# Values requested ahead of keys in the rounds, and one unit's keys and values requested by ScalarE

## The chip, the cores and the metric

The kernel runs on one core of a Trainium2 chip. The core has five engines that run their own instruction streams and meet at semaphores: TensorE (PE, matrix products), VectorE (DVE), ScalarE (ACT), GpSimd (POOL) and SyncE (SP), which here only requests transfers. Transfers between the chip's main memory and the core are carried by 16 DMA engines; an instruction on SP, ACT or POOL requests one. The metric is the device time of one execution in microseconds. Three runs of the kernel before took 182.39, 184.64 and 186.26 us; the median is 184.64.

## The reference

Two stages are chained: a retention layer (attention with a decay and no softmax), and a mixture of low-rank adapters on its output.

```python
batch, n_heads, seq, head_dim = 8, 8, 576, 64
scores = scale * q @ k.T                        # per batch and head
Dmat = where(rel >= 0, gamma[h] ** rel, 0)      # rel = row - column
x = ((scores * Dmat) @ v)                       # then to (4608, 512)
...
logits = x @ w_gate                             # (4608, 8)
topk = the 2 largest; w = softmax over the 2
out = x + sum over the 2 of w * (x @ A[e]) @ B[e]     # rank 16
```

## The kernel before

**Units.** The work is cut into 18 units. A full unit is one chunk of 128 positions of two batches with all 8 heads; a sequence of 576 positions has four full chunks and a tail of 64, and a tail unit takes the tails of four batches. Four batches give nine units (units 0 to 7 full, 8 a tail; 9 to 16 full, 17 a tail). Each unit needs its q, k and v, each as two transfers of 256 KB (`load`, L152, with `load_batch`, L139, for one of the two). The buffers rotate: three for q, four each for k and v (L136), so v of unit 4 goes into the buffer of v of unit 0.

**What is done with a unit.** `k_scale` (L223, on POOL) multiplies the keys by powers of the decay. `T_mm` (L243, PE) turns k and q; `k_out`, `q_out`, `qs_out` and `q_turn` (L257 to L287, mostly ACT, q_turn mostly POOL) put the turned tiles where the products need them (kT, M, Qs). `S1_mm` and `S0_mm` (L296, L313, PE) make scores within the chunk, and VectorE masks them (L357, L367). `U_mm` (L388, PE) multiplies keys and values of the chunk to the state (pu), which `U_out` (L404) adds to the state W of the next chunk. `W_values` and `V1_copy` (L209, L216, POOL) copy the values into W and V1. `O_mm` and `O1_mm` (L420, L441, PE) make the output of the unit, `xT_out` (L460, DVE) scales it. The adapters follow: `Z_mm` (L483) gives logits and the low-rank product, `route_a`, `route_s`, `route_b` (L539 to L570) choose and weigh, `X_mm`, `Y_mm`, `B_mm` make the result, `osb_out` (L667) copies it out, `store` (L691) writes it to memory.

**What sets the order.** Nothing reorders instructions: each engine works through its own in the order in which the text issues them, and waits in that order. Units 0 to 3 are written out by hand (L803 to L955); then the loop of L961 runs rounds r = 2 to 16, in which the U product is that of unit r+1, the O products are those of unit r, and the turned k and q those of unit r+2. A request for a buffer is issued by `freed(u, nm)` (L171), which loads unit u + 4 (k, v) or u + 3 (q) where u was, and waits on SP until all readers of the old content are done. In a round SP gets, in this order, k of unit r+5 (L965), v of unit r+4 (L970), the store of unit r-1 (L1002) and q of unit r+5 (L1006), two transfers each. ACT requests a few early transfers itself (L857, L870), in between its copies.

Of the kernel before, what the change touches and what calls it, by code (L numbers as in the profile page):

```python
# [21 lines left out]
def kernel(  # L22
# [10 lines left out]
    nc = tc.nc  # L33
# [91 lines left out]
    def full(u):  # L125
        return units[u][0] < NFULL

    def behind(u):

        c, bp = units[u]  # L130
        if c + 1 < NFULL:
            return u + 2, 0
        return next(x for x in range(NU) if units[x] == (NFULL, bp // 2)), bp % 2
# [5 lines left out]
    def load_batch(u, nm, b, eng=None):  # L139

        c, bp = units[u]
        return (eng or nc.sync).dma_start(
            out=nat[(nm, u)][:, b * H : (b + 1) * H, :],
            in_=srcs[nm][2 * bp + b, :, 128 * c : 128 * c + 128, :].rearrange("h j d -> j h d"),
        )

    def load_open(u, nm):
        nat[(nm, u)] = iop.tile(
            [128, 2 * H, Dh], FP32, tag=nm + "32", name=nm + "32", bufs=NBUF[nm]
        )  # L150

    def load(u, nm):  # L152

        if u >= NU:
            return
        load_open(u, nm)
        c, bp = units[u]
        if full(u):
            for b in range(2):
                load_batch(u, nm, b)  # L160
            return
        for par in range(2):
            b = 4 * bp + 2 * par
            nc.sync.dma_start(
                out=nat[(nm, u)][HALF[par]],
                in_=srcs[nm][b : b + 2, :, 128 * c : 128 * c + 64, :].rearrange(
                    "b h j d -> j (b h) d"
                ),
            )

    def freed(u, nm):  # L171

        load(u + NBUF[nm], nm)
# [7 lines left out]
    def copy(eng, out, in_):  # L181
        if eng is nc.scalar:
            nc.scalar.copy(out=out, in_=in_)  # L183
        else:
            eng.tensor_copy(out=out, in_=in_)  # L185

    def add(eng, out, a, b):
        eng.tensor_tensor(out=out, in0=a, in1=b, op=ALU.add)  # L188
# [5 lines left out]
    def heads(tl, p):  # L194

        v4 = tl.rearrange("p (b a o) d -> p b a o d", b=2, o=2)
        return [v4[:, b, :, p ^ b, :] for b in range(2)]

    def W_open(u):
        n = 1 if full(u) else 2  # L200
        st[u]["W"] = [
            wk.tile([128, 2, 2, HP, Dh], FP32, tag=f"W{x}", name=f"W{x}", bufs=(5, 2)[x])
            for x in range(n)
        ]
        if units[u][0] == 0:
            for p in range(2):
                (nc.vector if u < 2 else nc.gpsimd).memset(st[u]["W"][0][HALF[p], p], 0.0)

    def W_values(eng, u, ps=(0, 1)):  # L209
        vt = nat[("v", u)]  # L210
        for x, w in enumerate(st[u]["W"]):
            for p in ps:
                for b, src in enumerate(heads(vt[HALF[x]], p)):
                    copy(eng, w[HALF[1 - p], p, b], src)
# [8 lines left out]
    def k_scale(eng, u, bs=slice(0, 2)):  # L223
        c = units[u][0]
        kt = nat[("k", u)].rearrange("p (b h) d -> p b h d", b=2)[:, bs]
        eng.tensor_tensor(  # L226
            out=kt, in0=kt,
            in1=gv[:, c, :].unsqueeze(1).unsqueeze(3).broadcast_to(
                (128, bs.stop - bs.start, H, Dh)
            ),  # L230
            op=ALU.mult,
        )

    def T_open(u, nm, tag):
        s = st[u]
        s["p" + nm] = bank(tag, [128, 2, HP, 2, 64], name=f"pt_{nm}")
        if nm == "q":
            s["M"] = wk.tile([128, 2, 2, HP, 128], FP32, tag="M", name="M", bufs=3)
            s["Qs"] = wk.tile([128, HP, 2, 64], FP32, tag="Qs", name="Qs", bufs=2)
        else:  # L240
            s["kT"] = wk.tile([128, 2, HP, 2, 64], FP32, tag="kT", name="kT", bufs=2)
# [29 lines left out]
    def q_turn(eng, u, p):  # L271

        s = st[u]
        copy(
            eng, s["M"][HALF[p], p, 1],
            s["Qs"][HALF[1 - p]].rearrange("p a r i -> p a (r i)"),
        )
# [126 lines left out]
    def U_out(u):  # L404
        s = st[u]
        us, x = behind(u)
        if "W" not in st[us]:
            W_open(us)
        new, old = st[us]["W"][x], s["W"][0]
        if units[u][0] == 0:  # L410
            for p in range(2):
                copy(nc.scalar, new[HALF[p], p], s["pu"][HALF[p]])
            return
        add(nc.vector, new[LO, 0], s["pu"][LO], old[LO, 0])
        pn = wk.tile([128, 2, HP, Dh], FP32, tag="pn", name="pn", bufs=2)
        copy(nc.scalar, pn[HI], s["pu"][HI])
        add(nc.gpsimd, new[HI, 1], pn[HI], old[HI, 1])
# [23 lines left out]
    def O1_mm(u):  # L441
        s = st[u]
        if not full(u):
            return
        vt = nat[("v", u)]
        for hp in range(HP):
            for b in range(2):
                for ho in range(2):
                    p = ho ^ b
                    vv = s["V1"][:, b, hp, :] if p == 0 else vt[HI, b * H + 2 * hp + ho, :]  # L450
                    mm(  # L451
                        s["px"][HALF[ho], b, hp, HI],
                        lhsT=vv,
                        rhs=s["S1"][HALF[p], b, hp, :],
                        start=False,
                        stop=True,
                        skip_group_check=True,
                    )
# [21 lines left out]
    def Z_open(u, tag="F"):  # L480
        st[u]["pz"] = bank(tag, [128, 2, ER + E], name="pz")
# [70 lines left out]
    def route_s(u, ns=(0, 1)):  # L552
        s = st[u]
        for n in ns:
            nc.scalar.activation(
                out=s["sg"][:, n, :], in_=s["pz"][:, n, ER : ER + E], func=AFT.Sigmoid,
                bias=s["ns"][:, n : n + 1], scale=2.0,
            )
# [310 lines left out]
    k_out(nc.scalar, 1)  # L869
    load_batch(2, "q", 0, nc.scalar)  # L870
    load_batch(2, "q", 1)
    for nm, u in (("v", 2), ("k", 3), ("q", 3), ("v", 3)):
        load(u, nm)
    freed(0, "k")
    freed(0, "v")
    T_open(1, "q", "R")
    T_mm(1, "q")
    freed(1, "q")
    q_out(nc.vector, 1, 0)
    q_out(nc.scalar, 1, 1)  # L880
    qs_out(nc.scalar, 1)
    for p in range(2):
        q_turn(nc.scalar, 1, p)
    W_values(nc.gpsimd, 1)
    V1_copy(nc.gpsimd, 1)
    Z_open(0)
# [5 lines left out]
            S0_mask(1, p, slice(b, b + 1))  # L892
    S1_mask(1)
    U_mm(1)
    freed(1, "k")
    U_out(1)
    k_scale(nc.gpsimd, 2)
    nc.gpsimd.dma_start(out=Bcat, in_=moe_B.rearrange("e r d -> (e r) d"))
    W_values(nc.gpsimd, 2)
# [1 line left out]
    k_scale(nc.gpsimd, 3)  # L901
    O_mm(1, "A")
    O1_mm(1)
    freed(1, "v")
    route_a(0)
    route_s(0)
    for b in range(2):
        xT_out(1, slice(b, b + 1))
    route_b(0)
# [51 lines left out]
    for r in range(2, END):  # L961
        nxt, nn = r + 1, r + 2
        if full(nxt):
            U_mm(nxt, "E" if r > 2 else "F")
        freed(nxt, "k")  # L965
        if full(nxt):
            U_out(nxt)
        O_mm(r)
        O1_mm(r)
        freed(r, "v")  # L970
        if full(nxt):
            xT_out(r)
        else:
            for b in range(2):
                xT_out(r, slice(b, b + 1))
        if full(nxt):
            S1_mm(nxt, "R")
            S1_mask(nxt)
        S0_mm(nxt)
        for p in range(2):  # L980
            S0_mask(nxt, p)
        X_mm(r - 1)
        zT_out(r - 1)
        Z_open(r)
        Z_mm(r)
        route_a(r)
        early = nn < NU and not full(nn)
        if not early:
            Y_mm(r - 1, "R")
        if nn < NU:  # L990
            if "W" not in st[nn]:
                W_open(nn)
            T_open(nn, "k", "A")
            T_mm(nn, "k")
            k_out(nc.scalar, nn)
        if early:
            Y_mm(r - 1, "R")
        route_s(r)
        B_mm(r - 1)
        osb_open(r - 1)  # L1000
        osb_out(nc.vector if nn < NU else nc.scalar, r - 1)
        store(r - 1)  # L1002
        if nn < NU:
            T_open(nn, "q", "S")
            T_mm(nn, "q")
            freed(nn, "q")  # L1006
            q_out(nc.scalar, nn, 0)
            q_out(nc.scalar, nn, 1)
            qs_out(nc.scalar, nn)
            W_values(nc.gpsimd, nn)  # L1010
            if full(nn):
                V1_copy(nc.gpsimd, nn)
            for p in range(2):
                q_turn(nc.gpsimd, nn, p)
            if nn + 1 < NU:
                k_scale(nc.gpsimd, nn + 1)
            if r < 2 * NFULL and r % 2 == 0:
                gx_of(r // 2 + 1)
        route_b(r)
# [81 lines left out]
```

## Time and profile before

| | |
|---|---|
| median of three runs | 184.64 us |
| the profiled execution | 181.67 us |
| its span (first to last recorded work) | 179.9 us |
| bytes moved, mean rate | 39.00 MB, 217 GB/s |
| TensorE clock granted, mean | 0.991 of full speed |
| transfers of v, k, q from issue to landing, median (SP's) | 4.9, 4.8, 5.2 us |
| start of the first round's U product (unit 3) | 33.79 us |
| start of the U products of units 9 to 16 | 87.19, 96.06, 105.11, 114.16, 123.27, 132.32, 141.75, 151.50 us |

The profile was taken from one execution, which was faster than the median of the other runs. Times in its rows are in microseconds from the start of the span. A row of a timeline gives start, length, engine, line, operation and operands, and in brackets how long the engine had stood idle before it and what ended that. SPq and ACTq are requests for transfers: their length is how long the issuing engine was held by the request, not how long the transfer took. The chain of work that ended last is followed back from the last instruction, at each step to what released it.

### The profile page before, as it was taken

What the parts mean: (1) busy time and instruction counts of PE and PEld (TensorE: products, weight loads), DVE (VectorE), ACT (ScalarE), POOL (GpSimd) and SP (SyncE); (2) the same over time, 40 slices, a digit from 0 to 9 for tenths busy, and PEclk for the clock granted to TensorE, in tenths of its full rate; (3) what the DMA queues carried; (4) which work ended last, traced back from release to release, by engine and by line L of the source; (5) the groups of instructions that cost most, each with busy time, mean ns of one, the idle gap of its engine ahead of it and who ended that gap; (6) DMA issues with size and microseconds to landing.
All of it is one profiled execution on the core that took longest, in us unless ns stands there. A gap on an engine that the chain in (4) does not pass through costs nothing.

```text
span 179.9 us, 9354 instructions
## 1 busy us (share of the span) xinstructions
PE 172.6 (96%) x4126; PEld 157.0 (87%) x4126; DVE 129.9 (72%) x236; ACT 77.5 (43%) x158; POOL 121.9 (68%) x208
## 2 busy tenths in 40 slices
PE   7999999999999999999999999999999998999990
PEld 5799988989999999988989999999998997989960
DVE  6586475788696869687595878787777767587860
ACT  0743644926262625261818170707171625243330
POOL 7990956597979597878985659595869492992000
PEclk9999999999999999999999999999999999999996
DMA  4999998998989798999989988899999788843126
GB/s 118 281 266 255 249 213 189 231 219 181 260 205 272 193 256 228 249 245 272 242 239 209 266 191 217 229 232 234 236 275 231 184 195 244 232 159 120 47 101 207
DMA packets 119368, 39.00 MB, mean 217 GB/s; under 512 B 114320, under 2 KB 114720, under 8 KB 119328
## 3 DMA queue, kind: packets, MB, share of 16 engines
q1 hardware_dynamic: 113360, 36.51, 81.7%
q10 hardware_dynamic: 5792, 1.75, 4.1%
q8 instruction: 32, 0.52, 1.2%
q0 software_dynamic: 176, 0.15, 0.6%
q14 instruction: 8, 0.07, 0.1%
HBM read 29.09 MB, written 9.44 MB: 214 GB/s over the span
## 4 chain that ended last, share of the span: by engine, by line
PE 91%; DMA 3%; DVE 2%; issue 0%; DVEq 0%
PE pz L487 19%; PE px L432 18%; PE pu L395 9%; PE ps L322 8%; PE pt_k L248 6%; PE px L451 6%; PE po L620 5%; PE pt_q L248 5%; PE ps L304 4%; PE po L605 4%; DMA v<-in_v_dram 3%; PE pf L723 3%; PE pzt L587 2%; DVE M L373 2%; PE pa L514 1%; PE ps L338 1%
## 5 line engine op out<-in xcount | busy, mean ns | idle before, releaser
L185 POOL COPY W<-v 64x256 f32<-64x256 f32 x78 | 29.2, 394 | 21.8 <-DMA v<-in_v_dram 18.7
L373 DVE TENSOR_TENSOR M<-ps,tri 64x1024 f32<-64x1024 f32 (+1 forms) x34 | 37.3, 1097 | 4.7 <-PE ps L322 4.0
L487 PE MATMUL pz<-AW,xT 128*128 128x136 f32 x288 | 37.7, 284 | 0.0
L432 PE MATMUL px<-M,W 128*64 128x128 f32 (+1 forms) x640 | 35.4, 263 | 0.4 <-DVE M L373 0.4
L487 PEld LDWEIGHTS pz<-AW,xT 128*128 128x128 f32 x288 | 34.6, 190 | 0.4
L226 POOL TENSOR_TENSOR k<-k,pack 128x1024 f32<-128x1024 f32 (+1 forms) x18 | 32.5, 1806 | 2.7 <-issue 1.1
L183 ACT COPY kT<-pt_k 128x1024 f32<-128x1024 f32 x17 | 17.3, 1016 | 37.6 <-PE pt_k L248 37.6
L432 PEld LDWEIGHTS px<-M,W 128*64 128x64 f32 x640 | 31.8, 137 | 0.8 <-issue 0.6
L185 POOL COPY M<-Qs 64x512 f32<-64x512 f32 x34 | 20.7, 609 | 12.1 <-ACT Qs L183 9.5
L470 DVE TENSOR_TENSOR xT<-px,gx 128x1024 f32<-128x1024 f32 x11 | 13.5, 1225 | 16.2 <-PE px L451 14.6
L185 DVE COPY osb<-po 128x1024 f32<-128x1024 f32 (+2 forms) x18 | 19.2, 1075 | 6.9 <-PE po L620 5.4
L596 ACT COPY zT<-pzt 128x256 f16<-128x256 f16 (+1 forms) x19 | 6.9, 361 | 36.9 <-PE pzt L587 36.9
L183 ACT COPY M<-pt_q 64x512 f32<-64x512 f32 x35 | 20.2, 577 | 1.5 <-PE pt_q L248 0.6
L395 PE MATMUL pu<-v,k 128*64 128x64 f32 x512 | 18.9, 226 | 0.6 <-DMA v<-in_v_dram 0.6
L322 PE MATMUL ps<-Qs,kT 64*64 64x128 f32 (+1 forms) x304 | 18.3, 260 | 0.0
L395 PEld LDWEIGHTS pu<-v,k 128*64 128x64 f32 x512 | 16.5, 137 | 2.0 <-DMA v<-in_v_dram 0.4
L322 PE MATMUL ps<-M,kT 64*64 64x128 f32 (+1 forms) x304 | 18.2, 259 | 0.0
L188 POOL TENSOR_TENSOR W<-pn,W 64x512 f32<-64x512 f32 x12 | 15.2, 1270 | 4.0 <-ACT pn L183 3.1
L322 PEld LDWEIGHTS ps<-M,kT 64*64 64x64 f32 x304 | 15.0, 134 | 0.3
L322 PEld LDWEIGHTS ps<-Qs,kT 64*64 64x64 f32 x304 | 14.9, 134 | 0.0
L248 PEld LDWEIGHTS pt_k<-ident,k 64*128 64x128 f32 x272 | 9.9, 138 | 3.2 <-issue 2.9
L185 POOL COPY V<-v 64x256 f32<-64x256 f32 x32 | 11.9, 399 | 0.7
(75 smaller groups left out, 297.5 us busy)
## 6 DMA issues: line engine op xcount, KB each, us to landing
v<-in_v_dram SPq DMA_DIRECT2D x36, 256.0 KB, 4.9
q<-in_q_dram SPq DMA_DIRECT2D x35, 256.0 KB, 5.2
out_dram<-osb SPq DMA_DIRECT2D x34, 256.0 KB, 4.8
k<-in_k_dram SPq DMA_DIRECT2D x33, 256.0 KB, 4.8
k<-in_k_dram ACTq DMA_DIRECT2D x3, 256.0 KB, 4.6
An<-in_moe_A_dram ACTq DMA_DIRECT2D x1, 256.0 KB, 4.4
q<-in_q_dram ACTq DMA_DIRECT2D x1, 256.0 KB, 4.9
out_dram<-osb ACTq DMA_DIRECT2D x2, 128.0 KB, 2.5
```

Source lines behind the costliest of these rows:

```text
L183: nc.scalar.copy(out=out, in_=in_)
L185: eng.tensor_copy(out=out, in_=in_)
L188: eng.tensor_tensor(out=out, in0=a, in1=b, op=ALU.add)
L226: eng.tensor_tensor(out=kt, in0=kt, in1=gv[:, c, :].unsqueeze(1).unsqueeze(3).broadcast_to((128, bs.stop - bs.start, H, Dh)), op=ALU.mult,)
L248: mm(ps[:, r, hp, b, :], lhsT=src[HALF[r], b * H + 2 * hp : b * H + 2 * hp + 2, :], rhs=ident[HALF[r], 64 * r : 64 * r + 64], is_transpose ...
L322: mm(s["ps0"][HALF[1 - p], b, hp, sl], lhsT=s["kT"][HALF[ho], x, hp, b, :], rhs=Q_of(u, b, ho, hp, sl), start=(hp == 0 and x == 0), stop=True,
L373: nc.vector.tensor_tensor(out=s["M"][sl, p, bs].rearrange("p b a i -> p (b a) i"), in0=s["ps0"][sl, bs].rearrange("p b a i -> p (b a) i"), ...
L395: mm(s["pu"][HALF[p], b, hp, :], lhsT=nat[("k", u)][:, h, :], rhs=nat[("v", u)][:, h, :], start=(hp == 0 and b == 0), stop=True, skip_grou ...
L432: mm(s["pxb"][b][HALF[ho], hp, sl], lhsT=s["W"][x][:, p, b, hp, :], rhs=s["M"][:, p, b, hp, sl], start=(hp == 0 and x == 0), stop=True, sk ...
L451: mm(s["px"][HALF[ho], b, hp, HI], lhsT=vv, rhs=s["S1"][HALF[p], b, hp, :], start=False, stop=True, skip_group_check=True,)
L470: nc.vector.tensor_tensor(out=s["xT"][:, bs].rearrange("p b a i -> p b (a i)"), in0=s["px"][:, bs].rearrange("p b a i -> p b (a i)"), in1= ...
L487: mm(s["pz"][:, n, :], lhsT=s["xT"][:, n, dt, :], rhs=AW[:, dt, :], start=(dt == 0), stop=(dt == HP - 1), skip_group_check=True,)
```

## The change

Two things are moved, and no work is added or taken away. In the rounds, the request for the values of unit r+4 stands ahead of that for the keys of unit r+5; both now stand behind the O products. In the part written out by hand, the keys and values of unit 3 are requested by ScalarE and no longer by SyncE: the two transfers of the keys behind its q copies of unit 1, one of the values behind the state copies of unit 1 (`U_out`), the other behind the sigmoids of unit 0 (`route_s`). SP's requests that stood between (k, v of unit 4, q of unit 4, k and v of unit 5) are written in one group behind `route_s(0)`, in the order v4, k4, q4, v5, k5; before it was k4, v4, q4, k5, v5.

```diff
@@ -869,18 +869,18 @@
     load_batch(2, "q", 0, nc.scalar)
     load_batch(2, "q", 1)
-    for nm, u in (("v", 2), ("k", 3), ("q", 3), ("v", 3)):
-        load(u, nm)
-    freed(0, "k")
-    freed(0, "v")
     T_open(1, "q", "R")
     T_mm(1, "q")
-    freed(1, "q")
     q_out(nc.vector, 1, 0)
     q_out(nc.scalar, 1, 1)
     qs_out(nc.scalar, 1)
     for p in range(2):
         q_turn(nc.scalar, 1, p)
+    load_open(3, "k")
+    for b in range(2):
+        load_batch(3, "k", b, nc.scalar)
+    load(2, "v")
+    load(3, "q")
     W_values(nc.gpsimd, 1)
...
     U_mm(1)
-    freed(1, "k")
     U_out(1)
+    load_open(3, "v")
+    load_batch(3, "v", 0, nc.scalar)
     k_scale(nc.gpsimd, 2)
...
     O1_mm(1)
-    freed(1, "v")
     route_a(0)
     route_s(0)
+    load_batch(3, "v", 1, nc.scalar)
+    freed(0, "v")
+    freed(0, "k")
+    freed(1, "q")
+    freed(1, "v")
+    freed(1, "k")
     for b in range(2):
         xT_out(1, slice(b, b + 1))
...
@@ -962,12 +968,13 @@
         if full(nxt):
             U_mm(nxt, "E" if r > 2 else "F")
-        freed(nxt, "k")
         if full(nxt):
             U_out(nxt)
         O_mm(r)
         O1_mm(r)
+
         freed(r, "v")
+        freed(nxt, "k")
         if full(nxt):
             xT_out(r)
```

## The prediction

> **What bounds the kernel now.** I read the profile's page first, then the waits, the chain of work that ended last, and the timelines of SP, POOL, ACT and PE around the places that the diff touches.
>
> ```profile
> PE 172.6 (96%) x4126; PEld 157.0 (87%) x4126; DVE 129.9 (72%) x236; ACT 77.5 (43%) x158; POOL 121.9 (68%) x208
> ...
> DMA  4999998998989798999989988899999788843126
> ...
> PE 91%; DMA 3%; DVE 2%; issue 0%; DVEq 0%
> ```
>
> TensorE is busy for 172.6 of 179.9 us and carries 91% of the chain. The DMA row stands at 8 or 9 tenths from the second slice to the thirty-first: the transfers are almost as full as TensorE. So reordering requests cannot remove work of either; it can only remove the moments in which TensorE stands for a transfer. The waits say which those are (columns: total us, times, longest):
>
> ```profile
> POOL W L185 <- DMA v<-in_v_dram: 18.7, 13, 4.0
> ...
> DVE osb L185 <- DMA out_dram<-osb: 1.4, 3, 0.7
> ...
> PE pu L395 <- DMA v<-in_v_dram: 0.6, 2, 0.3
> ```
>
> In the rounds only the values (v) are late: POOL stands for them 13 times (its W copies, off the chain), and PE's U product (pu, L395) twice. No row has PE standing for k or q. The chain, in order of time, and PE's own rows at the worst place:
>
> ```profile
> 28.30 1.08 PE pu L395 x32
> ...
> 29.60 0.62 PE ps L304 x32
> ...
> 32.57 0.72 PE pt_k L248 x16
> ...
> 114.16 1.15 PE pu L395 x32
> ...
> 132.32 1.08 PE pu L395 x32
> ...
> 141.75 1.21 PE pu L395 x32
> ...
> 145.87 6.22 DMA v<-in_v_dram
> 152.14 1.04 PE pu L395 x28
> ```
>
> ```profile
> 150.50 0.68 PE L248 MATMUL pt_q<-ident,q 64*128 64x64 f32 x16
> 151.50 0.34 PE L395 MATMUL pu<-v,k 128*64 128x64 f32 x4 [0.33 <-DMA v<-in_v_dram]
> 152.14 1.04 PE L395 MATMUL pu<-v,k 128*64 128x64 f32 x28 [0.30 <-DMA v<-in_v_dram]
> ```
>
> An undisturbed U block takes 1.08 us after the q turn before it. That of unit 16 should have ended at 150.50 + 0.68 + 1.08 = 152.26 and ended at 152.14 + 1.04 = 153.18: 0.92 lost. The block at 141.75 lost 1.21 - 1.08 = 0.13, that at 114.16 lost 0.07. Late values cost TensorE 1.12 us in this execution. It is little, but they land on the edge in every one of these rounds, so anything that slows the transfers goes into the time.
>
> **Part 1, the rounds: values ahead of keys.** A round requests two transfers each of k[r+5], v[r+4], a store and q[r+5], in that order. SP's rows (start, length, for the pair):
>
> ```profile
> 94.80 2.68 SPq L142 DMA_DIRECT2D k<-in_k_dram  x2
> 97.58 2.18 SPq L142 DMA_DIRECT2D v<-in_v_dram  x2
> ...
> 104.47 2.23 SPq L142 DMA_DIRECT2D k<-in_k_dram  x2
> ...
> 141.25 3.87 SPq L164 DMA_DIRECT2D k<-in_k_dram  x2
> 145.22 1.41 SPq L142 DMA_DIRECT2D v<-in_v_dram  x2
> ```
>
> Nothing is added or removed: 4 requests of a round change places. These are k12 and v11 of round 7, k13 of round 8, k17 and v16 of round 12. SP goes from one to the next without a gap and is far behind its own program: v11 is released by round 7, whose PE work ended near 87, and goes out at 97.58. So freeing is no longer what holds a request; the queue is, and the later release of v (it needs the O products of unit r, k only U) makes no new SP wait while SP lags. If that lag were gone, v would hold k, store and q behind it by about one O block, which costs nothing as the values would then be early.
>
> Values gain the keys' place: 97.58 - 94.80 = 2.78 us for v11, 145.22 - 141.25 = 3.97 for v16. Unit 16's second half landed at 145.87 + 6.22 = 152.09; 3.97 earlier is 148.1, and TensorE asks at 151.18: 3 us to spare. The losses of 0.92 + 0.13 + 0.07 go: -1.12 us.
>
> Keys lose the values' place: 2.2 us for k12, 1.5 for k17. Who waits for keys first is POOL's scaling:
>
> ```profile
> 24.05 1.17 POOL L185 COPY W<-v 64x256 f32<-64x256 f32 x3 [0.70 <-DMA v<-in_v_dram]
> 25.27 0.75 POOL L185 COPY V<-v 64x256 f32<-64x256 f32 x2
> 27.12 1.90 POOL L226 TENSOR_TENSOR k<-k,pack 128x1024 f32<-128x1024 f32 x1 [1.10 <-issue]
> ...
> 108.60 1.90 POOL L226 TENSOR_TENSOR k<-k,pack 128x1024 f32<-128x1024 f32 x1
> ...
> 155.40 1.90 POOL L226 TENSOR_TENSOR k<-k,pack 128x1024 f32<-128x1024 f32 x1
> ```
>
> ```profile
> k<-in_k_dram SPq DMA_DIRECT2D x33, 256.0 KB, 4.8
> ```
>
> k12's second request goes out by about 96.2 and by the median of 4.8 us lands near 101; unit 12 is scaled at 108.60: 7.6 to spare, 5.4 after. k17 lands near 143.2 + 6 = 149 against 155.40: 6 to spare, 4.7 after. Cost nothing, under a cover of 4 to 5 us; if that were gone, each late us would pass to the k turn on PE. Stores and q keep their places. Next late is then the values again (2 to 4 us spare), then the stores.
>
> **Part 2, the fourth unit's keys and values on ScalarE's queue.** Four requests leave SP (k3, v3) and go to ACT: two behind the turned q copies, one behind the W copies, one behind the sigmoids. ACT's rows:
>
> ```profile
> 11.95 0.47 ACTq L142 DMA_DIRECT2D k<-in_k_dram  x1
> ...
> 16.79 0.37 ACTq L142 DMA_DIRECT2D q<-in_q_dram  x1
> ...
> 19.23 1.25 ACT L183 COPY M<-Qs 64x512 f32<-64x512 f32 x2
> 21.94 1.17 ACT L183 COPY W<-pu 64x512 f32<-64x512 f32 x2 [1.46 <-PE pu L395]
> 24.22 0.43 ACT L555 ACTIVATE sg<-pz,ns 128x8 f32<-128x8 f32 x2 [1.11 <-DVE ns L547]
> 25.79 1.01 ACT L183 COPY kT<-pt_k 128x1024 f32<-128x1024 f32 x1 [1.14 <-PE pt_k L248]
> ...
> 27.89 0.59 ACT L183 COPY Qs<-pt_q 128x512 f32<-128x512 f32 x1
> ```
>
> An ACT request takes 0.37 to 0.47 us. Two (0.94) go into the gap of 1.46, one into 1.11, one into 1.14: cost zero, hidden by waits that ACT has anyway. The buffers are the fourth of four, never used, so the requests wait for nothing. SP's early order becomes v2, q3, v4, k4, q4, v5, k5; before it had these rows:
>
> ```profile
> 19.98 3.16 SPq L142 DMA_DIRECT2D k<-in_k_dram  x2
> 23.25 2.78 SPq L142 DMA_DIRECT2D q<-in_q_dram  x2
> 26.07 3.03 SPq L142 DMA_DIRECT2D v<-in_v_dram  x2
> ```
>
> v3 goes out near 23.1 and 24.7 instead of 26.07. k3 now travels beside v2 instead of behind it. Lower bound: v2 lands as before, at 24.05 where POOL's copies resume. Upper bound: its last 24.05 - 20.48 = 3.57 us take twice as long, 27.6. TensorE wants v2 at 28.30; POOL would then copy until 27.6 + 1.17 + 0.75 = 29.5 and scale k3 until 31.4, ahead of its turn at 32.57: covered at both ends, by 0.7 us at the worse. I take zero. The moved releases (v4, k4, q4, v5, k5) only change program text on a queue that is behind; their buffers are free before SP arrives.
>
> What two queues do for the rate no row shows directly; the nearest:
>
> ```profile
> 9.00:16.25 7.25, 7.25 (x190) 6.88 (x188) 5.98 (x9) 1.95 (x4) 4.18 (x8) 1.00 1.20 270
> 16.25:25.10 8.85, 8.49 (x211) 7.70 (x208) 4.35 (x9) 5.55 (x11) 6.09 (x12) 1.00 1.05 224
> ```
>
> With An and half of k2 on ACT's queue the stretch of 9 to 16 us moved 270 GB/s; that of 16 to 25, with one early ACT request, 224. If ACT's requests raised 8.5 us from 224 to 270, SP would be 8.5 x 46 / 224 = 1.7 us further on for good; if the engines are full either way, 0. The share of busy engines was above 1 in both stretches, which is nearer to full: I take 0 and leave 1.7 to the range. [...]
>
> **The sum.** The profiled execution took 181.67 (span 179.9 and 1.77 around it): 181.67 - 1.12 = 180.55. The median of the three runs, 184.64, lies 2.97 above it. The program's arithmetic is the same in each run, so the excess is in something that varies, and what varies in the trace are the transfers (a pair of requests takes from 1.41 to 3.87 us in the rows above). If all 2.97 is late values, 2.8 or more of it comes back, since the values are 2.78 to 3.97 earlier: 184.64 - 1.12 - 2.8 = 180.7. If none: 183.5. Without a row that decides I take about the middle, 182.2.
>
> **The rivals.** *More than that comes back:* the excess is all late values, or ACT's queue adds its 1.7 us of lead. Time 180.5. For it: the values sit on the edge from unit 11 on. Against: the equal work for the engines.
> *The wait only changes its name:* the transfers as a whole set the pace, and a slow run is then held by the stores, which keep their place (VectorE already stood 3 times for them, 1.4 us), or by keys, which come later. TensorE gets back almost nothing: 184.6. Against: the spare of 4 to 5 us for keys.
> *Slower:* ACT's queue is as clogged as SP's, and a request holds ACT as long as it can hold SP:
>
> ```profile
> L142 SPq DMA_DIRECT2D v<-in_v_dram x32: 367/930/2136, 5.7 to 145.9; - x32
> ```
>
> At the longest, 2.14 us, from 20.48: two requests to 24.76, W copies to 25.93, third to 28.07, sigmoids to 28.5, fourth to 30.64. The kT copy would start there and not at 25.79, Qs would end at 28.48 + 4.85 = 33.33, and S1 of unit 2, at 29.60 now, starts 3.7 late. With the gain of 1.12: 184.64 - 1.12 + 3.7 = 187.2. It decides from the point where kT is 1.12 + 1.12 = 2.24 late (the first 1.12 is the spare between Qs and S1), about 1.5 us a request. Against it: ACT's own rows of 0.37 and 0.47, taken while SP's pair rows were long.
>
> **How the numbers follow.** Forecast 0.50 (182.2, its own range 180.9 to 183.6); more 0.22; new name 0.18; slower 0.10. Two per cent, about what a measurement of this kernel tells from no change, puts the bounds at 180.95 and 188.33. Faster: the 0.22 and 0.03 of the forecast, 0.25. Slower: half of the last rival, whose price may come on a run without the gain, 0.05. The same: 0.70. The range, 180.0 to 185.2, leaves out the last rival and the low end of the first.
>
> **What would show it.** Right: no pu row with a wait for v from unit 11 on, U blocks of 1.08; POOL's 18.7 us of waits for v down to a few; on SP the v pair ahead of the k pair; k scaling with no wait; ACT requests under 0.6 us, kT of unit 2 still near 25.8; the 9 us pace of the rounds unchanged. Wrong: pu or W copies waiting as before, pt_k or pt_q waiting for transfers, VectorE's osb copy waiting for stores, ACT requests above 1.5 us, or a median that stays at 184 with a profile free of waits, which would say that the excess was never late values.

## The result, and the profile after

The changed kernel takes 184.6 us (median of 20 executions, 181.86 to 186.74), the kernel before beside it on the same chip 183.11 us (20 executions, 179.83 to 186.26): a ratio of 1.0127, with an interval of 1.009 to 1.0165. It is 1.3% slower; 182.2 us, 1.3% below the 184.64 us of before, was forecast. The ratios here and below leave out every execution more than 1.5% above the fastest of its kernel, here 10 of the 20 of the changed kernel and 11 of the 20 of the kernel before; by the medians of all executions the ratio is 184.6 / 183.11 = 1.008. The profiled execution took 184.25 us with a span of 182.5, against 181.67 and 179.9 before.

The page of the changed kernel first: busy time, transfers, queues, chain by engine.

```profile
PE 172.3 (94%) x4126; PEld 156.8 (86%) x4126; DVE 131.4 (72%) x236; ACT 77.6 (43%) x158; POOL 121.7 (67%) x208
...
DMA  5997999998899999989998999999999997303135
...
q1 hardware_dynamic: 109200, 35.46, 77.9%
q10 hardware_dynamic: 9952, 2.80, 6.6%
q8 instruction: 32, 0.52, 1.2%
...
PE 91%; DMA 2%; issue 2%; DVE 2%; SPq 0%; DVEq 0%
```

TensorE's busy time is nearly the old one (172.6 before), so its idle time grew from 179.9 - 172.6 = 7.3 to 182.5 - 172.3 = 10.2 us. One entry of the chain has grown: "issue" went from 0% to 2%. The page of the profile defines it as time in which an engine waited for nothing that the profile shows. The row of queue 8 (packets, MB, share of 16 engines) looks negligible; its packets turn out to land just ahead of where TensorE's stops end.

The waits of the changed kernel (total us, times, longest):

```profile
POOL M L185 <- ACT Qs L183: 24.3, 12, 3.4
...
POOL W L185 <- DMA v<-in_v_dram: 7.7, 2, 6.0
...
PE pa L514 <- issue: 1.5, 1, 1.5
...
PE ps L304 <- issue: 1.2, 2, 0.8
```

POOL's waits for values fell from 18.7 us in 13 places to 7.7 in 2, and no row has the U product (pu) wait for a transfer. That is what the first part was forecast to do. SP's rows show the order swapped, values ahead of keys:

```profile
94.30 2.68 SPq L142 DMA_DIRECT2D v<-in_v_dram  x2
97.02 2.96 SPq L142 DMA_DIRECT2D k<-in_k_dram  x2
...
137.62 3.55 SPq L142 DMA_DIRECT2D v<-in_v_dram  x2
141.26 2.38 SPq L164 DMA_DIRECT2D k<-in_k_dram  x2
```

The chain in order of time answers to the one shown of before:

```profile
14.76 1.52 issue
...
35.80 1.08 PE pu L395 x32
...
45.11 1.08 PE pu L395 x32
...
48.66 0.82 issue
...
59.16 0.35 issue
...
145.29 1.08 PE pu L395 x32
...
154.31 1.08 PE pu L395 x32
```

The last two U blocks now begin 154.31 - 145.29 = 9.02 us apart and are 1.08 long; before they began 151.50 - 141.75 = 9.75 apart, and the second, with its gaps, took 153.18 - 151.50 = 1.68. So the late values are gone. But the block that began at 141.75 begins at 145.29: more than came back at the end was lost long before, most of it at 14.76 (1.52), 48.66 (0.82) and 59.16 (0.35). Here is TensorE at the first two:

```profile
14.04 0.71 PE L514 MATMUL pa<-An,sel 64*128 64x128 f32 x8
16.28 0.94 PE L514 MATMUL pa<-An,sel 64*128 64x128 f32 x13 [1.52 <-issue]
...
48.38 0.28 PE L304 MATMUL ps<-M,kT 64*64 64x64 f32 x2
49.48 0.27 PE L304 MATMUL ps<-M,kT 64*64 64x64 f32 x1 [0.82 <-issue]
```

TensorE stops in the middle of a run of products of one kind, for 1.52 and 0.82 us, and the profile names no operand that it waits for. The stop at 14.76 cannot come from the change, for no request that the change moves has been reached by then (the first, ACT's for k3, stands at 20.92). It varies from execution to execution: three of the four further profiles of the same kernel (e3, e12, e15) do not have it, and one (e17) has 0.4 us of it.

**What TensorE waits for.** I took the 32 packets of queue 8 out of the trace (16,384 bytes each), numbered them from 0 (packet n goes with border n), and counted TensorE's pairs of weight load and product from the start. The idle times stand at pairs 219 + 126.6 n, n a whole number, 253 loads and products apart. TensorE has 8,344 rows in the trace, 8,252 loads and products and 92 others, mostly semaphore instructions; with these counted too, from 0, the four stops of the changed kernel in the lines below stand at rows 450, 1218, 1985 and 2497, which is 450 + 256 n within a row (n = 0, 3, 6, 8). I call these places borders. Lines worked out so (us; "gap" is the distance of the pair from the one before it, about 0.05 when undisturbed):

```
kernel         packet  border n-1   packet from .. to    pair  starts   gap   start - packet end
before              3     25.72      27.56 ..  28.51      600   31.72   0.09   3.22
before             24    131.59     133.87 .. 134.79     3260  136.20   0.37   1.40
before             26    142.03     143.18 .. 144.66     3514  146.07   0.21   1.41
after               0                13.91 ..  14.87      219   16.29   1.80   1.42
after               3     27.39      31.42 ..  32.30      598   33.79   0.48   1.49
after               6     44.07      46.52 ..  47.99      976   49.48   1.09   1.49
after               8     54.92      56.60 ..  58.19     1230   59.51   0.62   1.33
```

Each stop ends 1.3 to 1.5 us after a packet has landed, and where a packet landed 3.2 us ahead there was no stop. The page names queue 8 "instruction", and in these two profiles none of its packets lands less than 1.3 us before TensorE goes on at the packet's border. So I take a packet of queue 8 for the next 256 instructions of TensorE; no row names what is in it. In the two profiles it starts 0.2 to 4.0 us behind the previous border and takes 0.88 to 1.85 us. Between two borders lie 3.6 to 7.3 us; where it is about 4, the packet has no more than 2 us to spare. The kernel before stops at such borders too: of its rows here, two did, for 0.5 us together beyond the 0.05.

**The balance of the two profiles.** At each border I took the gap beyond the smallest that any profile of this study has there, where a packet landed less than 1.6 us ahead. In sum that is 3.97 us in the changed kernel (1.72 at pair 219, 0.40, 1.05, 0.59, and two small ones) and 0.70 in the kernel before. 3.97 - 0.70, less the 1.12 of late values, is 2.15 of the 2.6 us by which the spans differ; the rest I did not trace.

### The profile page after: what moved, and what is told of

Same layout as the page of the kernel before. It is cut to its first block, busy times and chain, and to the rows that moved or that the text cites. A ratio compares the mean times of both kernels' runs of the same rounds, so it can differ in the third digit from the quotient of the medians.

```text
span 182.5 us, 9352 instructions
## 1 busy us (share of the span) xinstructions
PE 172.3 (94%) x4126; PEld 156.8 (86%) x4126; DVE 131.4 (72%) x236; ACT 77.6 (43%) x158; POOL 121.7 (67%) x208
## 4 chain that ended last, share of the span: by engine, by line
PE 91%; DMA 2%; issue 2%; DVE 2%; SPq 0%; DVEq 0%
PE pz L487 19%; PE px L432 17%; PE pu L395 9%; PE ps L322 9%; PE pt_k L248 6%; PE px L451 5%; PE po L620 5%; PE pt_q L248 5%; PE ps L304 4%; PE po L605 4%; DMA q<-in_q_dram 2%; PE pzt L587 2%; DVE M L373 2%; PE pa L514 1%; PE ps L338 1%
## 5 line engine op out<-in xcount | busy, mean ns | idle before, releaser
L395 PE MATMUL pu<-v,k 128*64 128x64 f32 x512 | 18.4, 225 | 0.0
```

The costliest lines, as they stand in the source:

```text
L395: mm(s["pu"][HALF[p], b, hp, :], lhsT=nat[("k", u)][:, h, :], rhs=nat[("v", u)][:, h, :], start=(hp == 0 and b == 0), stop=True, skip_grou ...
```

## The experiments

**The theories.** With the two profiles in hand I had these: *rounds* (moving the values costs something that the profile hides), *ScalarE's queue* (four requests from a second queue crowd the transfers, or hold ACT), *early order* (v4 ahead of k4), *instruction packets* (TensorE's own instructions come late beside full data queues, and the change makes this worse), and *chance* (a single profile of each kernel tells nothing). The last column counts the requests for unit 3 that ACT issues.

| run | kernel | median us | before beside it | ratio | interval | ACT's |
|---|---|---|---|---|---|---|
| e1 | rounds swapped alone | 180.79 | 181.05 | 0.9993 | 0.9961 to 1.0026 | 0 |
| e2 | hand-written part alone | 183.1 | 181.05 | 1.0064 | 1.0023 to 1.0105 | 4 |
| e3 | changed kernel again | 183.51 | 181.05 | 1.0141 | 1.0092 to 1.019 | 4 |
| e4 | kernel before again | 181.37 | 181.05 | 1.0006 | 0.9969 to 1.0043 | 0 |
| e5 | ACT's requests alone | 182.36 | 181.04 | 1.0113 | 1.0073 to 1.0152 | 4 |
| e6 | early order alone | 181.62 | 181.04 | 1.004 | 1.0001 to 1.0078 | 0 |
| e7 | changed, few stores | 181.92 | 181.04 | 1.0035 | 0.9989 to 1.008 | 4 |
| e8 | before, program shifted | 187.54 | 181.04 | 1.0379 | 1.0345 to 1.0413 | 0 |
| e9 | changed, nothing by ACT | 181.18 | 181.9 | 0.9997 | 0.9958 to 1.0037 | 0 |
| e10 | keys alone by ACT | 181.84 | 181.9 | 0.9985 | 0.9939 to 1.0031 | 2 |
| e11 | values alone by ACT | 180.96 | 181.9 | 0.9953 | 0.9921 to 0.9985 | 2 |
| e12 | changed kernel, third profile | 182.23 | 181.9 | 1.0056 | 1.0017 to 1.0095 | 4 |
| e13 | rounds swapped, values by ACT | 180.95 | 181.25 | 0.9976 | 0.9942 to 1.0011 | 2 |
| e14 | values alone by ACT, again | 181.56 | 181.25 | 0.9997 | 0.9957 to 1.0037 | 2 |

Four further profiles, one execution each: the changed kernel 182.61 (e15) and 182.1 (e17), the kernel before 180.55 (e16) and 180.43 (e18).

### Which part costs: e1 to e4

e1 swaps the rounds alone:

```diff
             U_mm(nxt, "E" if r > 2 else "F")
-        freed(nxt, "k")
         if full(nxt):
...
         O1_mm(r)
+
         freed(r, "v")
+        freed(nxt, "k")
```

> The rounds part alone (values ahead of keys), the hand-written part as before. Theory A (the early requests on ScalarE's queue hold up TensorE in the first 60 us; the rounds part does what was forecast): faster than before by 0.5 to 1.5 us, no U product waits for values from unit 11 on, U of unit 4 near 43. Theory B (values ahead of keys is what costs): slower than before by 1 to 2 us, with new stalls after 60 us.

e2 has the hand-written part of the change alone, and the rounds as before.

> The hand-written part alone (keys and values of unit 3 from ScalarE, the releases regrouped), the rounds as before. Theory A: slower than before by 2 to 3 us, TensorE idle without a releaser several times before 60 us, U of unit 4 near 45. Theory B: like before within 0.5 us.

e3 and e4 are the changed kernel and the kernel before, profiled once more.

> The changed kernel once more, for a second profile. If its idle time of 1.5 us at 14.8 us, which lies ahead of every instruction that the change touches, belongs to this program, it is there again; if it is chance of one execution, it is gone, and U of unit 4 comes about 1.6 us earlier than the 45.1 of the first profile. Time 1 to 2 us above before under both theories.

> The kernel before once more, for a second profile and as a measure of what a repetition moves: ratio 1 within 0.5%. Theory A: few and short idle times of TensorE without a releaser before 60 us (under 0.5 us in sum).

The rounds cost nothing and bring nothing: 0.9993, neither the gain of 0.5 us or more nor the loss of 1 us or more that the two theories named. The hand-written part is slower, 1.0064, and its interval leaves 1 out. The whole is again slower than before, 1.0141. The second profile of the kernel before (e4) shows why the swap brings nothing; its waits, and SP's request for the values of unit 16:

```profile
POOL W L185 <- DMA v<-in_v_dram: 4.4, 2, 4.0
...
PE ps L304 <- issue: 1.0, 1, 1.0
```

```profile
137.50 2.88 SPq L142 DMA_DIRECT2D v<-in_v_dram  x2
```

The kernel before, unchanged, waits for values in 2 places here and not in 13; both lie early, and no U product waits. The values of unit 16 were requested at 137.5 us and not at 145.2. The third and fourth profile of before (e16, e18) have no U product waiting for values either, nor have the seven profiles of other kernels that keep the rounds as they were (e2, e5, e6, e8, e10, e11, e14). The late values that I costed at 1.12 us were those of one execution in eleven.

### ScalarE's requests or the order: e5 and e6

e5 has ACT's four requests, and SP's releases in the order of before. e6 has everything on SP, with v4 ahead of k4 and v5 ahead of k5. e5 differs from e2 in this:

```diff
     load_batch(3, "v", 1, nc.scalar)
-    freed(0, "v")
     freed(0, "k")
+    freed(0, "v")
     freed(1, "q")
-    freed(1, "v")
     freed(1, "k")
+    freed(1, "v")
```

> Keys and values of unit 3 requested by ScalarE as in the change, the other early requests in the order of before (k4, v4, q4, k5, v5), rounds as before. If the second queue is what costs: slower than before by 1 to 2 us, as the whole early part was. If the order of the early requests costs: like before within 0.5 us.

e6, against the kernel before:

```diff
-    freed(0, "k")
     freed(0, "v")
+    freed(0, "k")
...
     U_mm(1)
-    freed(1, "k")
     U_out(1)
...
     freed(1, "v")
+    freed(1, "k")
```

> All early requests stay on SyncE; only the order v4, k4 and v5, k5 of the change in place of k4, v4 and k5, v5; rounds as before. If the second queue costs: like before within 0.5 us. If the order costs: slower by 1 to 2 us.

ACT's requests alone cost 1.0113, about what the whole change costs. The order alone gives 1.004, with an interval that begins at 1.0001 and so only just leaves 1 out, and as part of e9 below it costs nothing. So the cost lies with ACT's four requests.

### The instruction packets: e7 and e8

e7 leaves out the stores of units 1 to 13 of the changed kernel, so that fewer transfers are in the queues:

```diff
-        store(r - 1)
+        if r > 14:
+            store(r - 1)
```

> The changed kernel without the stores of units 1 to 13 (their rows of the output are not written): 26 of 36 output transfers fewer, all of TensorE's work kept. If TensorE's idle times without a releaser are its own instructions arriving behind data transfers: they all but vanish (under 0.5 us in sum after 50 us), the packets that fetch instructions start within 1 us of the block before, and the time falls to 180 to 181 us on a chip where the changed kernel takes 183.5. If the idle times have another cause: they stay, and the time stays within 1 us of the changed kernel.

e8 adds pairs of products ahead of everything, so that the borders fall on other work of the kernel before:

```diff
-    fill(5, "F")
+    fill(20, "F", 64)
```

> The kernel before with its 5 wide warm-up products replaced by 20 narrow ones of about the same time in sum, which puts 30 more pairs of weight load and product ahead of all else: every later instruction lies 30 pairs further on in TensorE's program. If the idle times without a releaser come at borders of 256 instructions of that program, they still come at pairs 219 + 126.6 k counted from the start, so 30 pairs earlier in the work than before. If they belong to a place in the work (a wait the profile does not name), they stay at the same work. Time within 0.5% of before under both.

From the packets and pairs as above:

```
kernel               packet  border n-1   packet from .. to    pair  starts   gap   start - packet end
e8 (before, shifted)      5     41.09      43.76 ..  44.68      850   46.14   0.63   1.46
e8 (before, shifted)     19    111.41     113.21 .. 114.14     2626  115.54   0.41   1.39
e7 (few stores)          15     87.92      89.42 ..  91.29     2119   92.61   1.01   1.32
e7 (few stores)          24    133.51     135.18 .. 136.34     3260  137.88   0.13   1.53
```

In e8 all work stands 30 pairs later in the program, and the stops are again at 219 + 126.6 n (850 is 219 + 126.6 x 5 less 2, 2626 is 219 + 126.6 x 19 plus 2). They belong to the place in the program, not to the work there. In time, e8 was a miss: I expected no change beyond the added pairs, and its first U product began 5.7 us later (16.53 and not 10.81). The first filling products, which took 8.80 us and not 4.64, make up 4.2 of it. Why they took longer isn't known, and e8's time is not used for anything.

e7 decides nothing. Its ratio to the kernel before is 1.0035, where the changed kernel has 1.0127, 1.0141 and, below, 1.0056, but its interval overlaps that of the last, and 181.92 us misses the 180 to 181 expected. Behind 50 us its borders cost 1.1 us and not the 0.5 expected at most: at 92.6 us it stops for 1 us as others do. From 93 us on they cost 0.1 us in sum, but three of the five profiles of the changed kernel (the result's, e12, e17), with all their stores, have no more there: 0 to 0.1. That data transfers hold the packets back is not shown; leaving out 26 of the 36 output transfers also frees buffers and SP.

### How many requests by ScalarE: e9 to e14

e9 is the whole change, with all of unit 3 requested by SP again:

```diff
-    load_open(3, "k")
-    for b in range(2):
-        load_batch(3, "k", b, nc.scalar)
     load(2, "v")
+    load(3, "k")
     load(3, "q")
+    load(3, "v")
...
-    load_open(3, "v")
-    load_batch(3, "v", 0, nc.scalar)
...
-    load_batch(3, "v", 1, nc.scalar)
```

> The change without ScalarE: all four requests of unit 3 back on SyncE (v2, k3, q3, v3, v4, k4, q4, v5, k5), values ahead of keys in the rounds. Theory A (ScalarE's second queue is the whole cost): like before within 0.5%, 3.1 to 3.3 transfers in flight from 16 to 30 us, no idle time of TensorE at a code border before 60 us. Theory C (the order in the rounds and in the start costs too): slower by 0.7% or more.

e10 is e2 with the values back on SP, e11 is e2 with the keys back on SP.

> Only the keys of unit 3 by ScalarE, its values by SyncE, rounds as before. If the cost is more transfers in flight ahead of TensorE's instructions: slower by about half of what the whole early part cost (0.3 to 0.7%), with 3.7 to 4 in flight from 16 to 30 us. If the cost is ScalarE held by its fourth request: like before within 0.3%, because no request stands ahead of the kT copy.

> Only the values of unit 3 by ScalarE, its keys by SyncE, rounds as before. The second half of the values still waits on ScalarE ahead of the kT copy. If that hold is the cost: slower by 0.5 to 1.1%, kT of unit 2 later than 26 us. If the number in flight is: 0.3 to 0.7%, with kT where it was.

> The changed kernel a third time, as a control on the same chip: 1.2 to 1.5% above before. Its profile should again show above 4 transfers in flight from 16 to 30 us and the fetches of instructions of that stretch landing later than in the kernel before (2.5 us behind the border).

e13 is e11 with the rounds swapped; e14 is e11 once more.

> The change with the keys of unit 3 back on SyncE: values of unit 3 by ScalarE, values ahead of keys in the rounds. If the parts add up as measured: 0.3 to 0.6% faster than before. If only the number in flight counts (3.8 in the start): like before.

> The values of unit 3 alone by ScalarE, repeated. If the gain of 0.5% of the first time is real: ratio 0.993 to 0.998. If chance: 0.998 to 1.002 and the interval holds 1.

Without ACT's requests the change costs nothing: 0.9997. With two of them, keys or values, it also costs nothing. e11 looked like a small gain (0.9953), but its repetition e14 gives 0.9997 and e13 0.9976: no gain is established, and no version beats the kernel before. Neither account in the expectations of e10 and e11 came out: 3.8 transfers were in flight in both at no cost, and in e11 ACT was not held (kT of unit 2 at 25.83 us). With all four and all stores, each of the five comparisons (the result, e2, e3, e5, e12) lies above 1 with its whole interval, from 1.0056 to 1.0141. By the medians of all executions the five are 1.002 (e12) to 1.014 (e3). So the loss comes with the four requests together; that is shown, its size only roughly. Why, is less well shown.

e12 was a miss: 0.56% and not the 1.2 to 1.5% expected. It is the third profile of the changed kernel, and has 0.55 us at borders and a span of 179.0, less than the first profile of the kernel before. The loss isn't there in each execution.

### More profiles of the same two kernels: e15 to e18

> The changed kernel, a fourth profile. If late instructions are its cost: idle time of TensorE at borders of 256 instructions between 1 and 3 us in sum, of which most after 25 us. If the hold of ScalarE: kT of unit 2 starts 1 us or more behind its products and the products after it wait.

> The kernel before, a third profile: idle time at borders of 256 instructions under 1 us in sum, no wait of the U product for values unless the values are requested later than 145 us for unit 16.

> The changed kernel, a fifth profile. If late instructions are its cost: idle time of TensorE at borders of 256 instructions between 1 and 3 us in sum. If the hold of ScalarE: kT of unit 2 starts 1 us or more behind its products and the products after it wait.

> The kernel before, a fourth profile: idle time at borders of 256 instructions under 1 us in sum; 3.1 to 3.4 transfers in flight from 16 to 30 us.

The borders of these four came out as expected of late instructions: 2.12 (e15) and 2.18 us (e17) with the change, 0.51 (e16) and 0.46 (e18) without it.

All profiles together but e7's and e8's, grouped by the number of ACT's requests for unit 3. "In flight" counts the transfers between the end of the request and landing from 16 to 30 us, "transfer" is their median time from the start of the request to landing, "packet" is how far behind the previous border packets 2 and 3 landed, "borders" is the sum worked out as in the balance above.

```
ACT's   profiles                                in flight    transfer    packet        borders, us
0       before e4 e16 e18 e1 e6 e9              3.1 to 3.4   4.9 to 5.5  2.3 to 3.1    0.46 to 2.50, mean 1.15
2       e10 e11 e13 e14                         3.8 to 3.9   5.2 to 5.4  2.2 to 3.1    0.45 to 2.01, mean 1.11
4       result e2 e3 e5 e12 e15 e17             4.2 to 4.5   5.4 to 6.2  2.6 to 4.4    0.55 to 3.97, mean 2.40
```

The means of the borders differ by 2.40 - 1.15 = 1.25 us between none and four. With the border near 15 us left out, which lies ahead of anything changed, it is 2.10 - 1.10 = 1.0. The loss by the comparisons is 0.56 to 1.41% of 181 us, 1.0 to 2.6 us. The stops at borders are thus of the size of the loss's smaller end. But single profiles scatter by 2 us or more, and seven a side is few. If seven of the 18 sums were drawn at random, their mean would lie as far above that of the others as that of the seven with four requests does in 0.4% of the draws.

The same sums can be set against the spans of the 18 profiles:

```
ACT's   span, mean   borders, mean   span less borders: mean, lowest, highest
0         179.56         1.15            178.41   178.15   179.20
2         179.35         1.11            178.24   177.76   178.71
4         181.06         2.40            178.67   178.15   179.21
```

The spans run from 178.2 to 182.5 us, over 4.3 us; with the stops at borders taken off, only 1.5 us of that is left. Spans and border sums go together with a correlation of 0.95. Of the 1.5 us between the groups of none and of four, 1.25 stand at borders and 0.26 elsewhere. The two largest remainders belong to the two profiles in which TensorE waits longest for something else besides: before (179.20, with the 1.12 us of late values) and e5 (179.21, with 1.03 us for which ACT keeps TensorE, shown below). So where the time of these profiles differs, it differs mostly by TensorE's stops at borders.

The rate between 16 and 30 us, from the windows of e4 (before) and of e12 (changed): us, then busy time and number of instructions of PE, PEld, DVE, ACT and POOL, the granted clock, the share of DMA engines, GB/s.

```profile
16.00:30.00 14.00, 13.64 (x327) 12.48 (x324) 7.78 (x18) 8.58 (x16) 10.08 (x17) 1.00 1.07 237
```

```profile
16.00:30.00 14.00, 13.64 (x320) 12.48 (x322) 7.76 (x18) 8.50 (x16) 9.43 (x16) 1.00 1.19 263
```

A second queue did raise the rate, 237 to 263. By 24 us the kernels with four requests had 27 or 28 issued (the result's, which had stopped at 15 us, 26) against 25 or 26 with none. By 40 us the lead was gone (38 to 40 against 37 to 39); what used it up was not shown. And TensorE's busy time in the stretch is 13.64 in both: it waited for none of the data that now came earlier. What did come later, in the mean, were packets 2 and 3 of queue 8: 3.26 against 2.53 us behind the border; without the result's profile and e2, 2.87.

**What stays open.** Only the result's profile and e2 stop at pair 598, right behind the crowded stretch. Up to packet 9, and without the first border, the four-request profiles lose 0.42 us in the mean and those without 0.04; behind that, 1.68 against 1.06. So most of the difference in e3, e5, e15 and e17 comes after 60 us, above all at pairs 2119 (0.91 us in the mean against 0.53) and 2372 (0.36 to 0.64 in three of seven, never without ACT's requests), where the number of transfers in flight is the same in all groups (3.2 to 3.4). How four early requests could act so late was not found. That the four requests cost something, 0.6 to 1.4% by the ratios, is shown, and that in the profiles most of the longer span is stops at borders is shown too. How four early requests bring these stops about, and whether the executions that were not profiled lose their time in the same way, stays open.

## Why the prediction was wrong

The forecast of 182.2 us had three terms against 184.64: -1.12 us for late values, about -1.3 us for a part of the median's excess that was to come back, and 0 for ScalarE's four requests. Measured, the first two are nought (e1: 0.9993), and the third is +0.6 to +1.4%, 1.0 to 2.6 us (e2, e5 and the changed kernel). The failed step is the third, the price of nothing for ScalarE's requests: it turned the sign. That 184.6 lies within the range of 180.0 to 185.2 is luck, as that range was laid around a gain.

**Part 1, the mechanism: right.** The values go out ahead of the keys, the U blocks are 1.08 long with no wait, POOL's waits for values fell to two early ones, and TensorE waits for neither keys nor stores in their place. (Of the 13 waits that I put into the rounds, three lie before 36 us; e4 has only two without the swap.) Its worth was wrong: "Late values cost TensorE 1.12 us in this execution" is true of that execution and of no other of the four of before. In the other three, SP was not so far behind: the values of unit 16 were requested at 137.5 to 140.8 us and not at 145.2. The gain measured is nought (e1, 0.9993).

**The term for the excess of the median: wrong.** The median of three lay 2.97 us above the profiled execution, and I took "about the middle" between all of it coming back and none, on the ground that transfers are what varies. No row bore that out. With 20 executions the median of before was 183.11 on that chip, and 181.04 to 181.9 on the later ones, with profiles at 180.43 to 181.53 (e4, e16, e18) in which TensorE waits for no late value. What made the first three long was never caught in a profile and stays open. What does vary from execution to execution, and was in the trace of before, is the idle time at the borders: 0.70 us in that profile, 0.46 to 1.58 in the other three of the same kernel.

**The step "the requests wait for nothing": wrong, but a small part of the loss.** The buffers were free, as I said. The requests still waited, as ACT's rows of the changed kernel show:

```profile
21.98 0.37 ACTq L142 DMA_DIRECT2D k<-in_k_dram  x1
23.62 0.58 ACT L183 COPY W<-pu 64x512 f32<-64x512 f32 x1 [1.46 <-PE pu L395]
23.62 0.60 ACTq L142 DMA_DIRECT2D v<-in_v_dram  x1
...
25.90 0.43 ACT L555 ACTIVATE sg<-pz,ns 128x8 f32<-128x8 f32 x2 [1.11 <-DVE ns L547]
27.26 0.38 ACTq L142 DMA_DIRECT2D v<-in_v_dram  x1
27.68 1.01 ACT L183 COPY kT<-pt_k 128x1024 f32<-128x1024 f32 x1 [1.36 <-PE pt_k L248]
```

The sigmoids end at 26.33, and the fourth request goes out at 27.26. In the trace each request names a semaphore, by whose counts the landing of its transfer is told. There are eight of them for SP and ACT (in the profiles of the result and of before 107, 109 and 112 to 117, for 18 or 19 requests each), taken in turn by the requests of both together (the next use is mostly the eighth request on, and 5 to 10 requests on in all 18 profiles). In none of the 18 profiles does a request go out before the earlier transfer of its semaphore has landed (the closest is 0.02 us behind it in the changed kernel's first profile and 1.20 us in the first of before), so it appears to wait for that landing. For three of ACT's requests (issue, and landing of the earlier transfer on the same semaphore):

```
kernel   request            issued   semaphore   earlier transfer on it      landed
after    k3, second half     21.98      112      k2, by SP at 17.36           21.96
after    v3, second half     27.26      116      v2, by SP at 20.56           27.24
e5       v3, second half     27.12      117      q3, by SP at 20.90           27.10
```

Each was issued 0.02 us behind that landing. Of ACT's requests for unit 3, two or three are as close in each profile with four of them but e2's (none there), one in e10, and none in e11, e13 and e14. The profile puts the hold down to other things: above, the kT copy appears to wait for pt_k. In e5 the same hold reaches TensorE; ACT's rows, then PE's:

```profile
24.16 0.43 ACT L555 ACTIVATE sg<-pz,ns 128x8 f32<-128x8 f32 x2 [1.19 <-DVE ns L547]
27.12 0.38 ACTq L142 DMA_DIRECT2D v<-in_v_dram  x1
27.54 1.01 ACT L183 COPY kT<-pt_k 128x1024 f32<-128x1024 f32 x1 [2.95 <-DMA q<-in_q_dram]
```

```profile
28.10 1.15 PE L395 MATMUL pu<-v,k 128*64 128x64 f32 x32
30.28 0.27 PE L587 MATMUL pzt<-ident,zc 128*128 128x128 f16 x2 [1.03 <-ACT Qs L183]
```

ACT stood for 2.5 us ahead of the request, kT came at 27.54 and not at 25.79, and TensorE lost 1.03. This is the third rival's place (the fourth request holds the turned keys of unit 2) by another cause than a clogged queue: its requests took 0.37 to 0.60 in the changed kernel's first profile, as forecast, and at most 0.98 in the others. In the other profiles with four requests the hold was 0 to 1.1 us and reached TensorE in none, so it isn't what makes them slower in the mean.

**The failed step: "cost zero" and "I take 0" for ScalarE's requests.** I bounded the effect of the second queue by 0 and a gain of 1.7 us, and considered no loss but that of ACT held by its requests. Measured, the four cost 1.0 to 2.6 us; in the profiles with them the span is 1.5 us longer in the mean than in those without, of which TensorE stands 1.25 us at borders. No row of mine had the packets of queue 8 in it. The rate rose nearly as far as the upper bound supposed (263 GB/s in e12 against 237 in e4, over 14 us), and the lead was worth nothing: TensorE is busy for 13.64 of these 14 us in both.

**The other points.** v2 and k2 were in time, as bounded. The early order costs about nothing (e6, e9). Of the signs named for "wrong", none appeared but the last, a slow median with a profile free of data waits, which I had said would mean that the excess was never late values. It did mean that: e1 takes the late values away and gains nothing. The rival that "more comes back" is refuted by e1; "the wait only changes its name" is nearest to what happened, in that TensorE now stands at borders, not for stores or keys as that rival had it. That its 184.6 us is the measured time is coincidence, as the kernel before took 183.11 beside it.

## What to carry to other kernels

A wait seen in one profile is worth its time only if it is there in a second profile of the same kernel: take the price of a change from what repeats, and do not hand the distance between a profile and a median to the one wait that the profile happens to show. When a stream of products stops in the middle with "issue" as its releaser, compare the place with multiples of 256 of TensorE's rows (here 450 + 256 n) and with the packets of the queue that the page names "instruction" (here each stop ended 1.1 to 1.5 us after one had landed). An engine that has work on the path should not be given requests for transfers merely because it has a gap and the buffer is free: look for which transfer last used the semaphore that its request names (here two of four requests went out 0.02 us behind the landing of that transfer), and what stands behind the request.

## What the hardware showed that I had not expected

- Beside the data, the queue that the page names "instruction" (queue 8) moved 32 packets of 16,384 bytes in an execution, by the places of the stops one for every 256 of TensorE's rows. A packet starts up to 4.4 us behind the previous border, lands 0.9 to 2.5 us later, and where TensorE stands for it is used 1.1 to 1.5 us after that; a late one stops TensorE by up to 1.8 us (e15, at pair 2119). At most borders TensorE does not stand; the others cost 0.45 to 3.97 us in an execution of some 180.
- Four requests from a second queue raised the rate of transfers between 16 and 30 us to between 257 and 267 GB/s (e2, e3, e5, e12, e15, e17; 244 in the result's profile), against 220 to 240 with none (before, e1, e4, e6, e9, e16, e18). Each transfer took longer, 5.4 to 6.2 us against 4.9 to 5.5.
- Two executions of one kernel differ by several us in how far SP runs ahead: the values of unit 16 were requested at 145.2 us in one profile of the kernel before and at 137.5 in another.
